# Where the modulation of a normalised input is applied: on the input's rows, or on the filter's weights with a rank-one shift

## The chip, the cores and the metric

The kernel runs on one core of one Trainium2 chip. The metric is the device time of one execution in microseconds (us); lower is better. A core has engines that run their own instruction streams in order and wait for each other by semaphores: TensorE (PE in the profile; PEld is its weight load), VectorE (DVE), ScalarE (ACT), GpSimd (POOL) and SyncE (SP, which here only issues DMAs).

## The reference

The kernel computes one block of a network in float32 on 2048 positions of 512 columns. The part that matters here is its first half: a layer norm of `u` is modulated by column vectors `ca` and `sa`, run through a long convolution whose kernel K is built from 128 complex states a column (S4), given a skip term, and added back under a gate `ga`.

```python
mod = (_silu(c) @ w_mod).reshape(c.shape[0], 6, 1, -1)
sa, ca, ga, sb, cb, gb = (mod[:, 0], ..., mod[:, 5])
h = _layernorm(x, axis=-1) * (1 + ca) + sa
x = x + ga * _A_ref(h, ...)
...
# _A_ref: K[d, l] = Re sum_n C[d,n] exp(dt[d] A[d,n] l) dt[d] B[d,n]
#         y = causal convolution of h with K (by FFT) + h * Dskip
```

The second half (a spatial shift mixer and a channel MLP) is not touched by the change. All of `ca`, `sa`, `ga` are one row of 512 numbers: they depend on the column, not on the position. The convolution and the skip are linear and act on each column by itself.

## The kernel before

The convolution is done as a Fourier transform in three stages: a 32-point transform over one index of the position, a twiddled 64-point one, a product of spectra, and the way back. The code runs in stages, each written out in order by hand (no scheduler moves instructions between or within engines; the order of the code is the order of each engine's queue). The stage of this case is a loop of 32 steps k, between the preparation of the constants and the second transform stage. It does two things side by side:

- **The filter.** For eight groups t of 64 columns (the `k // 4` of the code) and four quarters it builds the convolution kernel's partial sums. `turns(k)` computes phases on TensorE (L458, L459: two row halves of the array at once, 18 matmuls for a step), and ScalarE takes their sine and cosine (tile `tr`). `exps(t)` computes magnitudes: TensorE (L257, L252), then ScalarE's exponential. It is called in the steps with k % 4 == 1, and needs two loads of ScalarE's function table; there, a few filler matmuls (L492) stand between, and a dummy sine (`turn1`) brings the sine table back. `products(k)` multiplies magnitudes and phases on VectorE (L476, L482, L485, L486; tiles e, m). `burst(k)` sums over the states on TensorE (L508: 64 small matmuls into PSUM tile `kp`), and ScalarE copies every second `kp` into `KX`. The weight of each state, `WN`, enters by `weigh(t)` (L264), one multiplication of a quarter of the magnitudes' factors.
- **The input.** For each of 16 row blocks b, `u_stats` takes mean and variance on VectorE and the inverse root on GpSimd, and `u_norm` normalises and modulates in place by two instructions on VectorE (L425, L426). For every second block and each of two halves cp2, `u_dft` does the 32-point transform on TensorE (L435) into two PSUM banks; ScalarE copies them out (tile `vs`) and SyncE's queue writes them to DRAM (`VU`).

Step k emits, in this order: the copies left over from the step before; `turns(k + 2)`; the first two `exps` where there are any; `products(k)`; `burst(k)`; the rest of the `exps` with fillers; then the side work that a table assigns to the step (`side[k]`): norms, statistics, transforms. Block i is normalised in step 1 + 28 i // 16, its statistics two steps earlier, its transforms one and two steps later. Buffers tie the engines together: the phases use two PSUM buffers (`psx`), the sines three (`tr`), the products two, and the transforms of u share two PSUM banks (`psu`) with a few others.

Ahead of the loop, `mod_parts` and `mod_sum` make the column vectors `mods[0..2]` = sa, 1 + ca, ga, the same in all 128 partitions, in the order ca, ga, sa. The state weights are computed in `wn`, transposed on TensorE into a PSUM bank `wps`, and copied to `WN` by ScalarE. In step 1 the gate is multiplied into the scale and the shift (L584, L585), so that u comes out as ga (1 + ca) LN(u) + ga sa. The skip weights lie in four rows of the tile `DS` and are added into the filter's first tap at the end of the loop (`add_skip`).

Of the kernel before, what the change touches and what calls it, by code (L numbers as in the profile page):

```python
# [7 lines left out]
F32 = mybir.dt.float32  # L8
F32R = mybir.dt.float32r
# [18 lines left out]
def shape_constants():  # L28
    f = lambda x: np.ascontiguousarray(x.astype(np.float32))
    k1, k2, q = np.arange(32), np.arange(64), np.arange(32)  # L30
    c2b = lambda c: np.where(c < 32, 31 - c, c)
    th = 2 * np.pi * (k1[None] + .5) * q[:, None] / 64
    W = np.stack([np.cos(th), -np.sin(th)], 1)
    FU = np.zeros((4, 32, 2, 2, 2, 32))
    for h in range(2):
        for cp2 in range(2):
            cp = 2 * h + cp2
            FU[1 - cp if cp < 2 else cp, :, h, cp2] = W
    FU = FU.reshape(128, 2, 2, 2, 32).transpose(0, 1, 2, 4, 3)
    FK = np.zeros((2, 2, 32, 2, 64))  # L40
    FK[:, 0, :, 0] = FK[:, 1, :, 1] = W.reshape(32, 64)
    b = c2b(np.arange(64))
    al = 2 * np.pi * b[:, None, None] * ((k1[None, :, None] + .5) / 4096 + k2[None, None, :] / 64)
    c, s = np.cos(al), np.sin(al)
    T2 = np.stack([np.stack([c, -s], 2), np.stack([s, c], 2)]).reshape(128, 32 * 128)
    T3 = np.stack([s, -s]).reshape(128, 32 * 64)
    h, cq, cp2 = np.meshgrid(np.arange(2), np.arange(16), np.arange(2), indexing='ij')
    b = c2b((2 * h + cp2) * 16 + cq).reshape(64)
    al = 2 * np.pi * b[None, :] * k2[:, None] / 64
    c, s = np.cos(al), np.sin(al)  # L50
    Gm = np.zeros((64, 2, 64, 2))
    Gm[:, 0, :, 0], Gm[:, 0, :, 1], Gm[:, 1, :, 0], Gm[:, 1, :, 1] = c, s, -s, c
    Gm = np.tile(Gm.reshape(64, 256), (2, 1))
    FI = np.zeros((2, 2, 32, 16, 2, 2, 32))
    for hh in range(2):
        for c2 in range(2):
            for cc in range(16):
                bb = int(c2b(np.array((2 * hh + c2) * 16 + cc)))
                th = 2 * np.pi * (k1[:, None] + .5) * (bb + 64 * q[None]) / 4096
                FI[c2, 0, :, cc, hh, bb // 16 - 2 * hh] = np.cos(th) * (2 / 4096)  # L60
                FI[c2, 1, :, cc, hh, bb // 16 - 2 * hh] = -np.sin(th) * (2 / 4096)
    eye = np.eye(16)
    j = np.arange(32)
    c0 = np.tile((eye[:, :, None] * (j + .5)).reshape(16, 512), (2, 1))
    C0 = np.zeros((2, 2, 32, 2, 512))
    C0[:, 0, :, 0], C0[:, 1, :, 1] = c0, c0
    C0 = C0.reshape(128, 1024)
    e1 = (eye[:, :, None] * j).reshape(16, 512)
    e2 = (eye[:, :, None] * np.ones(32)).reshape(16, 512)
    C1 = np.concatenate([e1, e1, e2, e2] * 2, 0)  # L70
    ex0 = np.concatenate([np.arange(31, -1, -1), np.arange(32, 64)])
    ex1 = np.concatenate([64 * np.arange(8), 512 * np.arange(4)])
    CE = np.concatenate([(eye[:, :, None] * ex0.reshape(2, 32)[:, None, None, :]).transpose(1, 0, 2, 3).reshape(16, -1),
                         np.zeros((16, 64 * NX1))], 1)
    CE = np.tile(CE, (8, 1))
    for u in range(4):
        CE[u * 32:u * 32 + 32, 1024 + u * 16 * NX1:1024 + (u + 1) * 16 * NX1] = \
            np.tile((eye[:, :, None] * ex1).reshape(16, -1), (2, 1))
    PA = np.zeros((2, 4, 16, 2, 2, 4, 2, 16))
    PB = np.zeros((4, 2, 16, 4, 4, 2, 4, 16))  # L80
    for e in range(16):
        for v in range(2):
            for u in range(4):
                for p in range(2):
                    PA[v, u, e, v, p, u, p, e] = 1
        for c in range(8):
            for p in range(4):
                PB[c // 2, c % 2, e, c // 4 * 2 + c % 2, p, 1 - c // 2 % 2, p, e] = 1
    return {k: f(v) for k, v in dict(
        FU=FU.reshape(128, 256), FK=FK.reshape(128, 128), T2=T2, T3=T3, G=Gm,  # L90
        FI=FI.reshape(128, 16 * 128), C0=C0, C1=C1, CE=CE, PA=PA.reshape(128, 512), PB=PB.reshape(128, 2048), ID=np.eye(128)).items()}


# [18 lines left out]
def body(ctx, tc, A):  # L112
# [86 lines left out]
    MG = ph.tile([128, 512], F32R, name="MG")  # L199
    ON = ph.tile([128, 3, 128], F32R, name="ON")  # L200
    WN = ph.tile([128, 512], F32, name="WN")
    modu = ph.tile([128, 3, 512], F32, name="modu")
    mods = [modu[:, k] for k in range(3)] + [modg[:, k] for k in range(3)]
    psx = a1.enter_context(pool("psx", bufs=2, space=PSUM))
# [80 lines left out]
    with tc.manual_schedule():  # L285
# [13 lines left out]
        for j in range(4):  # L299
            Y.dma_start(DS[32 * j:32 * j + 1], A["dk"][j:j + 1])  # L300
        Y.dma_start(FK, A["FK"])
        V.memset(cst, MAGIC)
        for r in (32, 96):
            V.memset(cst[r:r + 32], 1.0)
# [101 lines left out]
        V.tensor_mul(ws, ws, mn)  # L406
        V.tensor_add(wn, wn, ws)
        V.tensor_tensor(as4(wn), as4(wn), by(dt), op=OP.mult)
    pr.close()

    wml = a1.enter_context(pool("wml", bufs=1, reuse_waits="tile"))
# [10 lines left out]
    def u_norm(b):  # L422
        x = ut[b // 4][:, b % 4]
        mv, r = ul.pop(b)
        V.scalar_tensor_tensor(x, x, mv[:, 0, 0:1], mods[1], op0=OP.subtract, op1=OP.mult)  # L425
        V.scalar_tensor_tensor(x, x, r[:, 0:1], mods[0], op0=OP.mult, op1=OP.add)  # L426

    def u_dft(b, cp2):
        x = ut[b // 4]
        ps = [psu.tile([128, 512], F32, name="pu") for h in range(2)]  # L430
        for i in range(2):
            for h in range(2):
                q = 64 * (1 - i if h == 0 else i)
                j = slice(32 * JB[2 * h + cp2], 32 * JB[2 * h + cp2] + 32)
                T.matmul(ps[h][q:q + 64], FU[j, h, cp2 * 64:cp2 * 64 + 64], x[j, b % 4 + i],  # L435
                         start=True, stop=True, skip_group_check=True)

        def evict():
            vs = uv.tile([128, 2, 512], F32, name="vs")
            for h in range(2):  # L440
                act(vs[:, h], ps[h])
                c0 = h * 32 + cp2 * 16 + (14 - b if h == 0 else b)
                for i in range(2):
                    Y.dma_start(dram(VU, (c0 + i) * 256, [[16384, 64], [1048576, 2], [1, 256]]),
                                vs[i * 64:i * 64 + 64, h].rearrange("p (a d) -> p a d", a=2))
        later.append(evict)
# [22 lines left out]
    def products(k):  # L469
# [5 lines left out]
        for a in range(2):  # L475
            V.scalar_tensor_tensor(e0[:, 1, a], tr[:, 1, 0], 1.0 - 2.0 * a, mg[:, a], op0=OP.mult, op1=OP.mult)  # L476
        if k == 0:
            weigh(0)
        if u % 2 == 0:
            m1 = m1s[0] = wk1.tile([128, 2, 512], F32, name="m1")  # L480
# [59 lines left out]
    with tc.manual_schedule():  # L540
# [2 lines left out]
        wps = psu.tile([128, 512], F32, name="pu")  # L543
        for i in range(4):
            T.transpose(wps[:, i * 128:i * 128 + 128], wn[:, i * 128:i * 128 + 128], ident)
        act(WN, wps)
        late = mod_parts(2)
        turns(1, 0)
        late()
# [4 lines left out]
        for k in range(33):  # L554
# [26 lines left out]
                if k % 4 == 3 and k < 28:  # L581
                    weigh(k // 4 + 1)
            if k == 1:
                V.tensor_mul(mods[1], mods[1], mods[2])  # L584
                V.tensor_mul(mods[0], mods[0], mods[2])  # L585
            for f in side[k]:
                f()
        for f in later:
# [681 lines left out]
```

## Time and profile before

| | us |
|---|---|
| median of 3 runs | 716.0 (714.89 to 717.39) |
| the profiled execution | 714.44 |
| its span, first to last instruction | 712.6 |

| engine | busy us | share of the span |
|---|---|---|
| TensorE, matmul | 669.5 | 94% |
| TensorE, weight load | 516.9 | 73% |
| VectorE | 506.6 | 71% |
| ScalarE | 335.5 | 47% |
| GpSimd | 86.7 | 12% |

The profiled execution's own time is 1.8 us above its span. The shares are means over stages: the loop of this case lies between about 40 and 212 us, and after it come the second stage of the transforms and the matmuls of the second half. A row of the order of time reads: start in us, duration, engine, line, operation, output<-input, shape, count, and in brackets the idle time of the engine before it and what ended it. A row of a group reads: line, engine, operation, output<-input, shapes, xcount | busy us, mean ns of one | idle us before them, and who ended it. A row of the waits reads: engine, tile and line <- the one waited for: us in total, times, longest. A row of a stretch reads: from:to, its length, the busy time and count of each engine, the clock granted to TensorE (1.00 is full), the share of the DMA engines and GB/s.

### The profile page before, as it was taken

The page shows a single profiled execution, that of the slowest core. Times are in us where ns is not written, and L with a number is a line of the kernel's source. Part 1 is how long each engine was busy: PE and PEld are TensorE (multiplying, and loading weights), DVE is VectorE, ACT ScalarE, POOL GpSimd, SP SyncE. Part 2 cuts the span into 40 slices and gives each one's busy share as a digit, 9 for nine tenths or more (in the row PEclk, how much of TensorE's full clock was granted, in tenths as well). Part 3 has the DMA queues.
Part 4 walks back from the last instruction along what each step waited for, and adds up shares of the span by engine and source line. Part 5 has one row for each costly group of instructions (what it writes and reads, how often), then busy time and mean ns, then how long its engine had stood idle before and what let it go on. Part 6 is the DMA issues. An engine that isn't in the chain of part 4 may idle for free.

```text
span 712.6 us, 16838 instructions
## 1 busy us (share of the span) xinstructions
PE 669.5 (94%) x7083; PEld 516.9 (73%) x7083; DVE 506.6 (71%) x847; ACT 335.5 (47%) x549; POOL 86.7 (12%) x191
## 2 busy tenths in 40 slices
PE   2689999999999999998999899999999999999997
PEld 1256555656569665664688889999898988989896
DVE  8889999999996666866988868557464636454422
ACT  3769888889866444533344623314123221212120
POOL 1011211112000000000473100101010000000000
PEclk9899999999999999999999999999999999999999
DMA  8451374653439999874659201011020101111011
GB/s 280 145 144 52 91 218 101 181 139 94 141 75 332 237 301 302 267 241 152 204 176 319 90 22 39 16 45 31 27 63 16 53 22 31 31 30 30 0 30 30
DMA packets 56627, 85.51 MB, mean 120 GB/s; under 512 B 5508, under 2 KB 43400, under 8 KB 54888
## 3 DMA queue, kind: packets, MB, share of 16 engines
q1 hardware_dynamic: 52536, 66.87, 33.2%
q0 software_dynamic: 3136, 16.52, 6.5%
q8 instruction: 56, 0.92, 0.6%
q10 hardware_dynamic: 880, 1.05, 0.5%
q14 instruction: 19, 0.16, 0.1%
HBM read 58.20 MB, written 31.85 MB: 126 GB/s over the span
## 4 chain that ended last, share of the span: by engine, by line
PE 47%; DMA 2%; DVE 2%; ACT 1%; issue 1%; SPq 1%; ACTq 0%; DVEq 0%
PE pm L824 7%; PE pm L825 7%; PE pm L827 7%; PE pa L948 6%; PE pa L940 6%; PE pa L941 6%; PE ph L878 2%; PE ph L879 2%; PE ph L881 2%; PE pT L789 2%; DMA ld<-ZT 1%; DMA GD<-go 1%; PE pT L1138 1%; PE py L721 1%; DMA win<-GD 0%
## 5 line engine op out<-in xcount | busy, mean ns | idle before, releaser
L120 ACT ACTIVATE gh<-pm 128x512 fp32r<-128x512 f32 (+1 forms) x48 | 26.9, 561 | 200.6 <-PE pm L827 200.6
L824 PE MATMUL pm<-nh,w3h 128*128 128x256 f32 (+1 forms) x352 | 85.8, 279 | 0.9 <-ACT nh L120 0.9
L825 PE MATMUL pm<-nh,w3l 128*128 128x256 f32 (+1 forms) x352 | 85.6, 279 | 0.1
L932 DVE TENSOR_TENSOR gl<-gf,gh 128x512 fp32r<-128x512 f32 (+1 forms) x48 | 30.9, 643 | 68.3 <-ACT gf L120 68.3
L940 PE MATMUL pa<-w4h,gh 128*128 128x512 f32 (+1 forms) x176 | 69.6, 395 | 0.0
L941 PE MATMUL pa<-w4l,gh 128*128 128x512 f32 (+1 forms) x176 | 68.9, 392 | 0.0
L824 PEld LDWEIGHTS pm<-nh,w3h 128*128 128x128 f32 (+1 forms) x352 | 65.3, 185 | 2.6 <-ACT nh L120 1.1
L825 PEld LDWEIGHTS pm<-nh,w3l 128*128 128x128 f32 (+1 forms) x352 | 65.2, 185 | 2.2 <-DVE w3l L743 0.5
L827 PE MATMUL pm<-nl,w3h 128*128 128x256 f32 (+1 forms) x352 | 54.8, 277 | 0.0
L948 PE MATMUL pa<-w4h,gl 128*128 128x512 f32 (+1 forms) x176 | 48.1, 390 | 0.8 <-DVE gl L932 0.8
L458 PE MATMUL xx<-MG,ON 64*128 64x512 f32 x160 | 47.0, 389 | 0.0
L459 PE MATMUL xx<-MG,ON 64*128 64x512 f32 x160 | 47.0, 389 | 0.0
L827 PEld LDWEIGHTS pm<-nl,w3h 128*128 128x128 f32 (+1 forms) x352 | 46.6, 185 | 0.2 <-DVE nl L797 0.2
L752 POOL TENSOR_TENSOR rs<-mv,eps_t 128x1 f32<-128x1 f32 (+1 forms) x39 | 11.9, 306 | 278.0 <-DVE mv L758 266.1
L884 DVE TENSOR_TENSOR h<-h,ph 128x512 f32<-128x512 f32 x16 | 11.0, 688 | 45.1 <-PE ph L881 45.1
L476 DVE SCALAR_TENSOR_TENSOR e<-tr,p 128x512 f32<-128x512 f32 x64 | 41.1, 683 | 1.8 <-ACT tr L120 1.8
L120 ACT ACTIVATE z<-pz 128x512 f32<-128x512 f32 x32 | 17.4, 594 | 51.4 <-issue 21.7
L677 DVE TENSOR_TENSOR ma<-pk,us 128x512 f32<-128x512 f32 x32 | 21.9, 686 | 26.8 <-issue 15.8
L508 PEld LDWEIGHTS kp<-e,e 128*32 128x32 f32 x2048 | 30.1, 110 | 12.9 <-issue 7.2
L948 PEld LDWEIGHTS pa<-w4h,gl 128*128 128x128 f32 (+1 forms) x176 | 33.0, 188 | 8.3 <-DVE gl L932 1.2
L485 DVE TENSOR_TENSOR e<-tr,p 128x1024 f32<-128x1024 f32 x32 | 39.0, 1218 | 0.0
L486 DVE TENSOR_TENSOR e<-tr,m 128x1024 f32<-128x1024 f32 x32 | 39.0, 1218 | 0.0
(234 smaller groups left out, 1755.6 us busy)
## 6 DMA issues: line engine op xcount, KB each, us to landing
VU<-vs SPq DMA_DIRECT2D x64, 128.0 KB, 3.2
ld<-VU SPq DMA_DIRECT2D x16, 512.0 KB, 14.1
ZT<-z POOLq DMA_DIRECT2D x15, 512.0 KB, 7.1
ld<-ZT SPq DMA_DIRECT2D x12, 512.0 KB, 5.5
Dw<-in_w POOLq DMA_DIRECT2D x8, 688.0 KB, 4.7
xu<-in_u SPq DMA_DIRECT2D x16, 256.0 KB, 5.7
KX<-in_u SPq DMA_DIRECT2D x16, 256.0 KB, 12.3
GD<-go SPq DMA_DIRECT2D x16, 256.0 KB, 2.5
```

What stands on the lines that cost most here:

```text
L120: return S.activation(out, in_, f, bias=bias, scale=scale)
L458: T.matmul(x[:, :512], la, ma, start=(i == 0), stop=(i == len(ops) - 1))
L459: T.matmul(x[:, 512:], lb, mb, start=(i == 0), stop=(i == len(ops) - 1))
L476: V.scalar_tensor_tensor(e0[:, 1, a], tr[:, 1, 0], 1.0 - 2.0 * a, mg[:, a], op0=OP.mult, op1=OP.mult)
L485: V.tensor_mul(e0[:, 0], tr[:, 0, 0:1].to_broadcast([128, 2, 512]), mg)
L486: V.tensor_mul(e1.rearrange("p r d q -> p r (d q)"), tr[:, :, 1], m1s[0][:, u % 2:u % 2 + 1].to_broadcast([128, 2, 512]))
L824: T.matmul(p, wh[:, k, c], hi[k], start=(k == 0), stop=False)
L825: T.matmul(p, wl[:, k, c], hi[k], start=False, stop=False)
L827: T.matmul(p, wh[:, k, c], lo[k], start=False, stop=(k == 3))
L940: T.matmul(acc[i], gh[:m, e, s], W4h[:m, f], start=(f == 0), stop=False)
L941: T.matmul(acc[i], gh[:m, e, s], W4l[:m, f], start=False, stop=False)
L948: T.matmul(acc[i], gl[:m, e, s], W4h[:m, f], start=False, stop=(f == 10))
```

## The change

u is now only normalised: (u - mean) r, by one instruction of ScalarE with a scale and a bias per row; VectorE forms the bias, -mean r, in one 128x1 instruction (`lun`). What depends on the column goes elsewhere:

- The factor ga (1 + ca) is multiplied into the state weights and into the skip weights. `mods[2]` becomes ga (1 + ca) ahead of the loop; a zero of 1 + ca is replaced by 1e-12 first. `WN` is made by a multiplication on VectorE out of PSUM, in step 0, in place of ScalarE's copy ahead of the loop. The four rows of `DS` are multiplied in step 1.
- The shift becomes sa / (1 + ca), to be added to the normalised u. It is the same for all positions, so that its 32-point transform is an outer product of the column sums of the transform's matrix (`F1`, a new constant) with the shift's row. One matmul for each of the two banks of `u_dft` writes this outer product first, and the transform accumulates on top of it. To keep float32's digits in the fast matmul format, row and sums are split into a rounded part and a rest, in rows 0, 32 and 64 of `SHS` and `F1S`, so that one matmul over 96 rows sums three products.
- `shift_rows`, called in step 1 in place of L584 and L585, makes the shift: reciprocal, multiplication, ScalarE's rounded copies, VectorE's rests.

```diff
+    F1 = np.zeros((96, 128))
+    F1[::32] = np.tile(W.sum(0).T.reshape(64), 2)
...
+        Y.dma_start(F1, A["F1"])
...
         V.tensor_tensor(as4(wn), as4(wn), by(dt), op=OP.mult)
+        V.tensor_scalar(ws, mods[1], 0.0, 1e-12, op0=OP.is_equal, op1=OP.mult)
+        V.tensor_add(mods[1], mods[1], ws)
+        V.tensor_mul(mods[2], mods[2], mods[1])
...
     def u_norm(b):
         x = ut[b // 4][:, b % 4]
         mv, r = ul.pop(b)
-        V.scalar_tensor_tensor(x, x, mv[:, 0, 0:1], mods[1], op0=OP.subtract, op1=OP.mult)
-        V.scalar_tensor_tensor(x, x, r[:, 0:1], mods[0], op0=OP.mult, op1=OP.add)
+        nm = wk.tile([128, 1], F32, name="lun")
+        V.scalar_tensor_tensor(nm, mv[:, 0, 0:1], -1.0, r, op0=OP.mult, op1=OP.mult)
+        act(x, x, AF.Identity, scale=r[:, 0:1], bias=nm)
+
+    def shift_rows():
+        V.reciprocal(mods[1], mods[1])
+        V.tensor_mul(mods[0], mods[0], mods[1])
+        act(SHS, mods[0][:96])
+        V.tensor_sub(SHS[64:96], mods[0][64:96], SHS[64:96].bitcast(F32))
+        act(F1S, F1)
+        V.tensor_sub(F1S[32:64], F1[32:64], F1S[32:64].bitcast(F32))
 
     def u_dft(b, cp2):
...
+        for h in range(2):
+            T.matmul(ps[h], F1S, SHS, start=True, stop=False, skip_group_check=True)
         for i in range(2):
             for h in range(2):
...
-                         start=True, stop=True, skip_group_check=True)
+                         start=False, stop=True, skip_group_check=True)
...
         if k == 0:
+            by_d = lambda z: z.rearrange("p (b a c) -> p b a c", b=32, a=4)
+            V.tensor_mul(by_d(WN), by_d(wps), mods[2].rearrange("p (a b c) -> p b a c", a=4, b=32))
             weigh(0)
...
-        act(WN, wps)
...
             if k == 1:
-                V.tensor_mul(mods[1], mods[1], mods[2])
-                V.tensor_mul(mods[0], mods[0], mods[2])
+                shift_rows()
+                for j in range(4):
+                    r = slice(32 * j, 32 * j + 1)
+                    V.tensor_mul(DS[r], DS[r], mods[2][r, j * 128:j * 128 + 128])
```

The queues of the engines move at three places. The numbers behind a tile's name are those of buffers, and in the brackets stands which engine's signal an instruction waits for. The line numbers of the changed kernel are a little higher: L476 becomes L496, L486 becomes L508, L508 becomes L530, L435 becomes L455.

VectorE's queue in step 1, before: the last product of step 1, the two multiplications of the column vectors, the normalisation of block 0, and the first product of step 2.

```order
L486 TENSOR_TENSOR e_553<-tr,m_467 128x1024
L584 TENSOR_TENSOR modu<-modu 128x512
L585 TENSOR_TENSOR modu<-modu 128x512 [waits Activation_49]
L425 SCALAR_TENSOR_TENSOR xu<-xu,lum,modu 128x512 [waits DVE_49,PE_49]
L426 SCALAR_TENSOR_TENSOR xu<-xu,lur,modu 128x512 [waits DVE_49,Pool_49]
L476 SCALAR_TENSOR_TENSOR e_639<-tr,p_264 128x512 [waits PE_49,Activation_49]
```

The same place in the changed kernel:

```order
L508 TENSOR_TENSOR e_560<-tr,m_474 128x1024
L439 RECIPROCAL modu<-modu 128x512
L440 TENSOR_TENSOR modu<-modu 128x512 [waits DVE_49,Activation_49]
L442 TENSOR_TENSOR SHS<-modu,SHS 32x512 [waits Activation_49]
L444 TENSOR_TENSOR F1S<-F_113,F1S 32x128 [waits DMAHW1_49,Activation_49]
L608 TENSOR_TENSOR DS<-DS,modu 1x128 x3
L608 TENSOR_TENSOR DS<-DS,modu 1x128 [waits DMAHW7_49]
L435 SCALAR_TENSOR_TENSOR lun<-lum,lur 128x1 [waits Pool_49]
L496 SCALAR_TENSOR_TENSOR e_655<-tr,p_268 128x512 [waits PE_49]
```

Between the products of step 1 and step 2, VectorE now has eight instructions of the new shift and skip, two of which wait for copies of ScalarE, and then the 128x1 bias.

ScalarE's queue at the same place of the changed kernel, from the exponentials of step 1 (tiles p) over the table load and the dummy sine to the phases of step 4 (`tr`):

```order
L122 ACTIVATE p_610<-xx 128x1024 [waits DVE_49,PE_49]
L122 ACTIVATE p_548<-xx 128x768 [waits PE_49]
L122 ACT_TABLE_LOAD
L122 ACTIVATE turn_377<-hpi 128x1
L122 ACTIVATE SHS<-modu 96x512 [waits DVE_49]
L122 ACTIVATE F1S<-F_113 96x128 [waits DMAHW1_49]
L122 ACTIVATE xu<-xu,lun,lur 128x512 [waits DMAHW5_49,DMAHW4_49,DMAHW6_49,DMAHW3_49,DVE_49]
L122 ACTIVATE KX<-kp 128x8x64
L122 ACTIVATE tr<-xx 128x1024 [waits PE_49,Activation_49]
```

Before, KX followed the dummy sine at once; SHS, F1S and the normalisation of block 0 (`xu`) have moved in between, and behind them wait the sines of step 4.

TensorE's queue in step 3 of the changed kernel, from the burst to the phases of step 6:

```order
L530 MATMUL kp<-e_728,e_729 32x64 x32
L450 MATMUL pu<-SHS,F1S 128x512 x2
L455 MATMUL pu<-xu,FU 64x512 x4
L478 MATMUL xx<-C_105,T0S 128x512
L479 MATMUL xx<-C_106,T1S 128x512
```

The row with SHS and F1S is new, here and ahead of each of the other 15 transforms of u; the rows around it stand as before.

More of the change, by code (lines that the diff above doesn't have):

```diff
@@ L89, in shape_constants @@
     return {k: f(v) for k, v in dict(
-        FU=FU.reshape(128, 256), FK=FK.reshape(128, 128), T2=T2, T3=T3, G=Gm,
+        FU=FU.reshape(128, 256), F1=F1, FK=FK.reshape(128, 128), T2=T2, T3=T3, G=Gm,
         FI=FI.reshape(128, 16 * 128), C0=C0, C1=C1, CE=CE, PA=PA.reshape(128, 512), PB=PB.reshape(128, 2048), ID=np.eye(128)).items()}
@@ L201, in body @@
     WN = ph.tile([128, 512], F32, name="WN")
+    F1 = ph.tile([96, 128], F32, name="F1")
+    F1S = ph.tile([96, 128], F32R, name="F1S")
+    SHS = ph.tile([96, 512], F32R, name="SHS")
     modu = ph.tile([128, 3, 512], F32, name="modu")
```

## The prediction

> **What bounds the kernel now.** I first read the busy shares by stretches, to find the stage that the change touches: the loop over 32 steps, from about 45 to 212 us. The first row below is its middle, the other three are a spell near the start in which TensorE idled.
>
> ```profile
> core 0: us, PE busy (x) PEld busy (x) DVE busy (x) ACT busy (x) POOL busy (x), PEclk, DMA share, GB/s
> 60.00:200.00 140.00, 135.20 (x2364) 84.42 (x2364) 137.91 (x181) 125.02 (x150) 24.51 (x36) 1.00 0.49 133
> 27.57:30.99 3.42, 0.33 (x1) 0.30 (x2) 3.28 (x7) 3.39 (x6) 0.00 (x0) 1.00 0.00 0
> 30.99:34.40 3.41, 3.17 (x4) 0.67 (x2) 2.31 (x4) 0.91 (x3) 0.00 (x0) 0.50 0.17 43
> ```
>
> In 140 us VectorE is busy 137.9, TensorE 135.2, ScalarE 125.0. The share alone names VectorE, and the change takes work from it. Whether that pays depends on who waits for whom, so next come the order of time for one step and the table of waits. A step k on TensorE is: the phases of step k+2 (18 matmuls of L458/L459), the burst of 64 small matmuls (L508) that needs VectorE's products (L476 to L486) of step k, and in 16 of the steps one DFT of u (L435).
>
> ```profile
> 105.55 1.22 DVE L486 TENSOR_TENSOR e<-tr,m 128x1024 f32<-128x1024 f32 x1
> ...
> 107.12 0.49 PE L458 MATMUL xx<-C,T0S 64*128 64x512 f32 x1
> ...
> 108.84 0.39 PE L458 MATMUL xx<-MG,ON 64*128 64x512 f32 x1
> ...
> 109.07 0.39 PE L458 MATMUL xx<-C0N,T0S 64*128 64x512 f32 x1
> ...
> 109.38 1.10 PE L508 MATMUL kp<-e,e 128*32 128x64 f32 x64
> ...
> 110.42 1.09 PE L435 MATMUL pu<-xu,FU 32*64 32x512 f32 x8
> ...
> 111.43 0.50 PE L458 MATMUL xx<-C,T0S 64*128 64x512 f32 x1
> ```
>
> The burst of step 11 starts at 109.38, 2.6 us after VectorE finished its products (106.77): TensorE was not waiting for VectorE, it was busy with the phases. From 107.12 to 111.43 the step is 2.26 us of phases, 1.04 of burst, 1.01 of DFT, with no gap. The waits over 60 to 200 us say the same:
>
> ```profile
> ACT vs L120 <- PE pu L435: 5.0, 7, 1.5
> ACT tr L120 <- PE xx L459: 3.5, 6, 1.1
> PE xx L257 <- ACT tr L120: 2.7, 6, 0.5
> PE xx L458 <- ACT p L120: 1.0, 3, 0.3
> PE kp L508 <- DVE e L486: 0.7, 2, 0.4
> ```
>
> TensorE loses 0.7 us to VectorE in the whole stretch. It and VectorE are about equally loaded; TensorE is in order and nearly gapless. So what the change adds to TensorE counts in full, and what it takes from VectorE is worth next to nothing.
>
> **The change, term by term.**
>
> *Work taken from VectorE.* Sixteen pairs of normalisation go:
>
> ```profile
> L426 DVE SCALAR_TENSOR_TENSOR xu<-xu,lur,modu 128x512 f32<-128x512 f32 x16 | 12.0, 752 | 1.8
> L425 DVE SCALAR_TENSOR_TENSOR xu<-xu,lum,modu 128x512 f32<-128x512 f32 x16 | 11.9, 746 | 0.0
> L168 DVE SCALAR_TENSOR_TENSOR dt_p<-dt_p,dt_r 128x8 f32<-128x8 f32 x6 | 1.0, 166 | 0.2
> ```
>
> A pair is 1.5 us, the 128x1 instruction in its place about 0.17 (nearest: 128x8, 166 ns): 16 x 1.33 = 21.3 us less VectorE. On the path this is worth only the waits of bursts for products: 0.7 us as recorded, about 1.1 with what a wait adds before the record shows it. **Term: -1.1** (bounds 0 and -2).
>
> *Outer products on TensorE.* Each of the 16 DFTs gets two matmuls of 96 rows x 128 columns x 512 ahead of it. The nearest work is the filler (L492), the same size and also placed behind a burst:
>
> ```profile
> 55.16 1.10 PE L508 MATMUL kp<-e,e 128*32 128x64 f32 x64
> 56.19 0.96 PE L492 MATMUL kp<-CE,TES 128*128 128x512 f32 x3
> 57.08 0.73 PE L257 MATMUL xx<-CE,TES 32*128 32x512 f32 x2
> ```
>
> Three fillers hold the engine 0.89 us, from 56.19 to 57.08. Inside a run one phase pair follows another every 0.23 us (108.84, 109.07); two fillers are thus 0.89 - 0.23 = 0.66, the switch between tile shapes included. Low end: 2 x 0.23 = 0.46; high end 0.89. I take 0.66, since they too stand between a burst and a narrow matmul: 16 x 0.66 = **+10.5** (7.4 to 14.2). Nothing covers it, as the step above has no gap.
>
> *The stop in step 1.* After the products of step 1 VectorE now runs `shift_rows`: a reciprocal, a multiplication, then a subtraction that needs ScalarE's copy SHS. In ScalarE's order that copy stands behind the five exponentials of step 1, a table load and the dummy sine. Behind the waiting subtraction are queued on VectorE the F1S subtraction, four skip rows, the small instruction, and the products of step 2. The place before, in the order of time of VectorE, ScalarE and TensorE, and below them the prices:
>
> ```profile
> 51.13 0.68 DVE L584 TENSOR_TENSOR modu<-modu 128x512 f32<-128x512 f32 x1
> ...
> 53.86 1.29 DVE L476 SCALAR_TENSOR_TENSOR e<-tr,p 128x512 f32<-128x512 f32 x2
> ...
> 57.34 1.22 DVE L486 TENSOR_TENSOR e<-tr,m 128x1024 f32<-128x1024 f32 x1
> ...
> 60.82 1.28 DVE L476 SCALAR_TENSOR_TENSOR e<-tr,p 128x512 f32<-128x512 f32 x2
> ...
> 64.29 0.42 DVE L264 TENSOR_TENSOR p<-p,WN 128x256 f32<-128x256 f32 x1
> ```
> ```profile
> 61.98 0.20 ACT L120 ACTIVATE turn<-hpi 128x1 f32<-128x1 f32 x1
> 62.09 0.58 ACT L120 ACTIVATE KX<-kp 128x512 f32<-128x512 f32 x1
> ```
> ```profile
> 62.27 1.10 PE L508 MATMUL kp<-e,e 128*32 128x64 f32 x64
> 65.98 1.10 PE L508 MATMUL kp<-e,e 128*32 128x64 f32 x64
> ```
> ```profile
> L372 DVE RECIPROCAL tp_mx<-tp_mx 128x512 f32<-128x512 f32 x1 | 3.4, 3353 | 0.0
> L304 DVE MEMSET cst<- 32x512 f32 x2 | 1.0, 485 | 0.3 <-DVE cst L302 0.2
> L309 DVE MEMSET cst<- 1x128 f32 x6 | 1.0, 165 | 0.4
> ```
>
> VectorE would be done with reciprocal and multiplication (3.35 + 0.69) at about 55.5. ScalarE reaches SHS at 62.1, where KX stood, and needs 0.6: 62.7. Then the subtraction on 32 partitions (0.49 to 0.69, taken 0.65), F1S 0.2, four rows of 128 at about 0.2, the small instruction 0.17: the products of step 2 start at 64.5 instead of 53.86. They took 58.56 - 53.86 = 4.70, so they end at 69.2, and the burst that ran at 62.27 runs at 69.25: +7.0. Step 3 follows: small instruction, statistics (0.82) and products (60.82 to 64.29, 3.47) end at 73.7, while TensorE is ready at 69.25 + 1.03 + 2.3 = 72.6. Its burst moves from 65.98 to 73.75. In step 4 the products end at 78.65 and TensorE arrives at 78.7: the debt is paid, TensorE is the later one again and catches nothing up. **Term: +7.8.** Bounds: +4 (if VectorE's small instructions overlap and ScalarE gets there earlier) and +10.
>
> *The clock.* TensorE then idles some 7 us. The granted clock fell to 0.50 from 30.99 to 34.40, after the 3.42 us before it held only 0.33 of matmul; while it is low, matmuls take twice as long, up to 1.7 us lost, but the wait of step 3 (1.1 us) hides most. **Term: +0.5** (0 to 1.7). The Trainium skill (TensorE: Matmul & The Clock Gate, Part 1) states that after at least one idle window of about 3.4 us the clock is halved until a busy window has passed; the row agrees, one window long. By that rule alone the sum would have 1.7 in place of 0.5.
>
> *ScalarE.* It gets 16 normalisations of 128x512, about 0.6 us by the nearest row, and loses one eviction (WN) before the loop:
>
> ```profile
> L120 ACT ACTIVATE vs<-pu 128x512 f32<-128x512 f32 x32 | 17.5, 604 | 6.3 <-PE pu L435 6.3
> ```
>
> That is 9.6 us into 15 us of idle time per 140, much of it ScalarE waiting for the very DFTs that get longer by 0.66. It has slack where they stand (TensorE's waits for ScalarE, 2.7 + 1.0, sit at the exponentials). **Term: 0** (0 to +5).
>
> *Ahead of the loop.* Three more VectorE instructions on the columns (0.43 + 0.69 + 0.69) follow the weights, in an idle spell of 1.84 us:
>
> ```profile
> 38.00 0.69 DVE L408 TENSOR_TENSOR KX<-KX,dt_o 128x512 f32<-128x512 f32 x1
> 40.53 1.29 DVE L476 SCALAR_TENSOR_TENSOR e<-tr,p 128x512 f32<-128x512 f32 x2 [1.84 <-ACT tr L120]
> 42.19 0.43 DVE L264 TENSOR_TENSOR p<-p,WN 128x256 f32<-128x256 f32 x1 [0.37 <-ACT WN L120]
> ```
> ```profile
> 44.88 1.12 PE L228 MATMUL pu<-xu,sp 128*128 128x512 f32 x2 [1.66 <-ACT xu L120]
> ```
>
> WN is now VectorE's multiplication out of PSUM: about 0.3 later than ScalarE's copy. A burst here starts 3.7 us after its products (58.56 to 62.27 in step 2, below called the lead), which covers it; were that gone, 0.3. The PSUM bank is held until 42.5, and its next user on TensorE comes at 44.9. F1 is one small load more on SyncE's queue, early. **Term: 0.**
>
> *Sum.* -1.1 + 10.5 + 7.8 + 0.5 = +17.7. Behind the loop nothing absorbs it: the next stage starts from the loop's last result. Against the profiled execution's own 714.4 us that gives 732.1. The runs' median is 1.6 above it; I forecast **733**.
>
> **Rivals.**
>
> *VectorE is the bound (faster).* If TensorE's 135 us held hidden slack, the loop would follow VectorE: -21.3, plus 4.5 for `shift_rows` beyond the two multiplications it replaces and 0.3. ScalarE would stop the gain at 125.0 + 14 x 0.6 = 133.4 of 140, so -6.6 there: about 708. It decides if bursts start right at the end of their products; step 11 speaks against it with 2.6 us. The Trainium skill (Perfetto Trace Analysis, Identifying the Most-Contended Engine) holds that TensorE's headroom is judged by weight loads, not matmul time; at 84.4 of 140 it would name VectorE. The gapless step decides against it here. Chance 0.05.
>
> *The stop is absorbed.* Had VectorE's delay stayed under the 3.7 us of that lead, only 10.5 - 1.1 would remain: 725. The order of both engines speaks against it. Chance 0.12.
>
> *ScalarE becomes a second bound.* In the steps with exponentials its table loads and sines already hold TensorE up; eight normalisations fall in or beside them, 8 x 0.6 = +5: 738. Chance 0.13.
>
> **Numbers.** The main case has 0.68 (727 to 737 by its terms' bounds); 0.02 is left for no change. About 0.3% (2 us) is what a measurement of this kernel can tell. Faster 0.05, same 0.02, slower 0.93. The range 724 to 740 takes in the absorbed stop and the ScalarE case and leaves out the fast one and the joint extremes.
>
> **What would show it.** In the profile after: a TensorE gap of about 7 us near 62 us ended by VectorE's products, with VectorE idle from 55.5 to 62.7 waiting for ScalarE's SHS; steps with a DFT of about 4.95 us instead of 4.31; VectorE's share of the loop falling to about 80% with TensorE unchanged; the loop's last burst near 230 instead of 212. Wrong would be: no such gap, outer products that take under 0.4 us a pair, or bursts that start as soon as their products end.

## The result

The changed kernel takes 735.1 us (median of four runs, 732.6 to 737.7), against 715.7 us for the kernel before: the ratio is 1.0268, with a 95% interval of 1.0228 to 1.0309. The forecast was 733, within 724 to 740.

The profile after, first by the shares of busy time from step 2 to the end of the norms, then two stretches around the place where the prediction saw a stop.

```profile
core 0: us, PE busy (x) PEld busy (x) DVE busy (x) ACT busy (x) POOL busy (x), PEclk, DMA share, GB/s
60.00:217.00 157.00, 145.40 (x2391) 90.36 (x2390) 126.61 (x178) 135.98 (x167) 23.57 (x36) 0.98 0.41 118
62.20:67.95 5.75, 0.53 (x6) 0.10 (x2) 4.73 (x11) 3.50 (x8) 0.00 (x0) 1.00 0.00 1
67.95:74.78 6.83, 4.64 (x78) 3.88 (x80) 6.79 (x11) 2.19 (x3) 1.89 (x3) 0.50 0.29 99
```

VectorE has fallen from 98% of the loop (137.9 of 140) to 81% (126.6 of 157), and the loop has become longer. The stop in the order of time, VectorE first:

```profile
50.04 1.22 DVE L508 TENSOR_TENSOR e<-tr,m 128x1024 f32<-128x1024 f32 x1
51.18 3.35 DVE L439 RECIPROCAL modu<-modu 128x512 f32<-128x512 f32 x1
54.63 0.69 DVE L440 TENSOR_TENSOR modu<-modu 128x512 f32<-128x512 f32 x1
63.10 0.68 DVE L442 TENSOR_TENSOR SHS<-modu,SHS 32x512 fp32r<-32x512 f32 x1 [7.79 <-ACT SHS L122]
63.80 0.28 DVE L444 TENSOR_TENSOR F1S<-F,F1S 32x128 fp32r<-32x128 f32 x1
64.10 1.19 DVE L608 TENSOR_TENSOR DS<-DS,modu 1x128 f32<-1x128 f32 x4
65.32 0.16 DVE L435 SCALAR_TENSOR_TENSOR lun<-lum,lur 128x1 f32<-128x1 f32 x1
...
68.87 1.22 DVE L508 TENSOR_TENSOR e<-tr,m 128x1024 f32<-128x1024 f32 x1
```

ScalarE at the same place, where the copy SHS stands behind the exponentials (p; two more run just ahead of the first row), the table load and the dummy sine (turn):

```profile
58.22 2.82 ACT L122 ACTIVATE p<-xx 128x1024 f32<-128x1024 f32 x3 [0.15 <-PE xx L262]
61.05 1.28 ACT L122 ACT_TABLE_LOAD   x1
62.35 0.20 ACT L122 ACTIVATE turn<-hpi 128x1 f32<-128x1 f32 x1
62.46 0.61 ACT L122 ACTIVATE SHS<-modu 96x512 fp32r<-96x512 f32 x1
```

And TensorE, with the two outer products (L450) between burst and transform:

```profile
70.14 1.93 PE L530 MATMUL kp<-e,e 128*32 128x64 f32 x64 [7.42 <-DVE e L508]
...
75.55 1.10 PE L530 MATMUL kp<-e,e 128*32 128x64 f32 x64
76.58 0.73 PE L450 MATMUL pu<-SHS,F1S 96*128 96x512 f32 x2
77.25 1.09 PE L455 MATMUL pu<-xu,FU 32*64 32x512 f32 x8
...
80.56 1.10 PE L530 MATMUL kp<-e,e 128*32 128x64 f32 x64
```

VectorE stands still for 7.8 us until ScalarE has made SHS, and TensorE then stands still for 7.4 us until the products of step 2 are there. From 76.58 to 77.25 the two outer products hold TensorE 0.67 us.

Where the 19 us come from is read best from the start of the bursts (L508 before, L530 after), one a step, taken from the two traces:

| burst of step | before, us | after, us | later by | outer products before it | later by, without 0.67 us for each pair |
|---|---|---|---|---|---|
| 0 | 49.92 | 50.27 | 0.35 | 0 | 0.35 |
| 2 | 62.27 | 70.14 | 7.87 | 0 | 7.87 |
| 3 | 65.98 | 75.55 | 9.57 | 0 | 9.57 |
| 5 | 76.55 | 87.47 | 10.92 | 2 | 9.58 |
| 16 | 136.46 | 150.87 | 14.41 | 8 | 9.05 |
| 31 | 212.02 | 231.18 | 19.16 | 16 | 8.44 |

Nearly all of it arises in two ways: 9.6 us at once in steps 2 and 3, and then about 0.67 us at each transform of u. The fall of the last column from 9.58 to 8.44 comes for the most part at the bursts of steps 12 and 24 (0.42 and 0.48), where before the burst waited for VectorE's products, and otherwise in steps that have exponentials beside the transform, where a pair adds only some 0.47. Behind the loop the two kernels differ by less than 1 us (500.6 and 501.5 us to the end of the span).

### The profile page after: what moved, and what is told of

Same layout as the page of the kernel before. It is cut to its first block, busy times and chain, and to the rows that moved or that the text cites. A ratio compares the mean times of both kernels' runs of the same rounds, so it can differ in the third digit from the quotient of the medians.

```text
span 732.7 us, 16909 instructions
## 1 busy us (share of the span) xinstructions
PE 683.7 (93%) x7115; PEld 525.8 (72%) x7115; DVE 494.2 (67%) x841; ACT 346.9 (47%) x566; POOL 85.6 (12%) x191
## 4 chain that ended last, share of the span: by engine, by line
PE 46%; DMA 2%; DVE 2%; ACT 1%; issue 1%; SPq 0%; ACTq 0%; DVEq 0%
PE pm L847 7%; PE pm L848 7%; PE pm L850 7%; PE pa L971 5%; PE pa L963 5%; PE pa L964 5%; PE ph L901 2%; PE ph L902 2%; PE ph L904 2%; PE pT L812 2%; PE py L744 1%; DMA GD<-go 1%; PE pT L1161 1%; DMA ld<-ZT 1%; DMA win<-GD 0%
## 5 line engine op out<-in xcount | busy, mean ns | idle before, releaser
L496 DVE SCALAR_TENSOR_TENSOR e<-tr,p 128x512 f32<-128x512 f32 x64 | 41.1, 684 | 23.2 <-ACT tr L122 18.1
L478 PE MATMUL xx<-MG,ON 64*128 64x512 f32 x160 | 48.4, 399 | 0.0
L479 PE MATMUL xx<-MG,ON 64*128 64x512 f32 x160 | 48.2, 398 | 0.0
L530 PEld LDWEIGHTS kp<-e,e 128*32 128x32 f32 x2048 | 30.8, 112 | 19.4 <-DVE e L508 8.6
L530 PE MATMUL kp<-e,e 128*32 128x64 f32 x2048 | 36.1, 223 | 7.4 <-DVE e L508 7.4
L508 DVE TENSOR_TENSOR e<-tr,m 128x1024 f32<-128x1024 f32 x32 | 39.0, 1218 | 0.0
```

Source lines behind the costliest of these rows:

```text
L478: T.matmul(x[:, :512], la, ma, start=(i == 0), stop=(i == len(ops) - 1))
L479: T.matmul(x[:, 512:], lb, mb, start=(i == 0), stop=(i == len(ops) - 1))
L530: T.matmul(kp[32 * j:32 * j + 32, (k % 2) * 4 + g], e1[:, r, d], e0[:, r, :, d * 32:d * 32 + 32], start=(r == 0), stop=(r == 1), skip_grou ...
```

## The experiments

All ratios are to the kernel before, from runs on the same chip beside it. Where an experiment is told by its bursts, these are taken from its trace as in the table above.

### The two costs, taken away one at a time and together

The first run takes the wait out of VectorE's step 1: the rests are subtracted in step 2, the skip rows multiplied in step 5.

```diff
         act(SHS, mods[0][:96])
-        V.tensor_sub(SHS[64:96], mods[0][64:96], SHS[64:96].bitcast(F32))
         act(F1S, F1)
+
+    def shift_rests():
+        V.tensor_sub(SHS[64:96], mods[0][64:96], SHS[64:96].bitcast(F32))
         V.tensor_sub(F1S[32:64], F1[32:64], F1S[32:64].bitcast(F32))
...
             if k == 1:
                 shift_rows()
+            if k == 2:
+                shift_rests()
+            if k == 5:
                 for j in range(4):
```

> The subtractions of the two rests move from step 1 to step 2 and the four skip rows to step 5, so that VectorE no longer waits for ScalarE's copies ahead of the products of step 2; all else is as in the changed kernel. My theory: the stop costs 9.6 us (bursts of steps 3 to 5 stand 9.6 us late after the outer products before them are taken off), so the gap of TensorE near 62 us goes, and the time is 735.1 - 9.6 = 725.5 us (723 to 728), 1.4% over the kernel before. Rival, ScalarE: its 16 normalisations of 0.81 us lengthen the loop, and the stop only hides some of it; then less than 5 us come back, and the time is over 730.

Measured: 727.6 us, ratio 1.0188 (1.0132 to 1.0243), the profiled span 723.4 against 732.7: inside the range of 723 to 728, but 7.5 us come back and not 9.6. TensorE's order of time shows what is left:

```profile
62.26 1.10 PE L532 MATMUL kp<-e,e 128*32 128x64 f32 x64
65.03 0.50 PE L480 MATMUL xx<-C,T0S 64*128 64x512 f32 x1 [1.67 <-ACT tr L122]
...
68.22 1.10 PE L532 MATMUL kp<-e,e 128*32 128x64 f32 x64 [0.77 <-DVE e L510]
```

The burst of step 2 is back at 62.26, where it was before the change. The burst of step 3 is at 68.22 in place of 65.98, for two reasons. Ahead of its phases TensorE waits 1.67 us for sines of ScalarE (before the change 0.26, at the same place): in ScalarE's queue SHS, F1S and the normalisation of block 0 now stand ahead of them. And the burst itself waits 0.77 us for VectorE's products, since the wait for ScalarE's copy, which comes at 62.7 whatever VectorE does, has moved by one step:

```profile
58.97 1.22 DVE L510 TENSOR_TENSOR e<-tr,m 128x1024 f32<-128x1024 f32 x1
62.71 0.68 DVE L445 TENSOR_TENSOR SHS<-modu,SHS 32x512 fp32r<-32x512 f32 x1 [2.52 <-ACT SHS L122]
```

The second run leaves the outer products out (and with them the shift), and keeps the stop.

```diff
-        for h in range(2):
-            T.matmul(ps[h], F1S, SHS, start=True, stop=False, skip_group_check=True)
...
-                         start=False, stop=True, skip_group_check=True)
+                         start=True, stop=True, skip_group_check=True)
```

> The 32 outer products are left out (the shift is thus missing from the result); the stop in step 1 stays. My theory: they stand on a gapless TensorE, 16 x 0.67 = 10.7 us, so the time is 735.1 - 10.7 = 724.4 us (722 to 727). Rival, VectorE or ScalarE as the loop's bound: the outer products lie beside other work, and under 4 us come back, over 731.

Measured: 723.7 us, ratio 1.0137 (1.0069 to 1.0205), inside the range. By the medians 11.4 us come back; the steps with a transform take 4.31 us again where they took 4.98 (step 16). By the last burst it is 8.0 us (223.17 against 231.18): in step 10 of this trace the granted clock falls (0.82 from 107.5 to 117.0 us) and the burst comes 1.6 us later, which neither the kernel before nor the changed one shows. Without that it would be 9.6. The outer products stand nearly in full on TensorE.

The third run has both edits.

> Both of the two edits: no outer products (the shift is missing from the result) and the rests taken later. What is left of the change is VectorE's relief of 21 us and ScalarE's 16 normalisations. My theory: TensorE alone sets the loop, VectorE's relief is worth about 1 us and ScalarE's load nothing: 735.1 - 9.6 - 10.7 = 714.8 us (712 to 717), equal to the kernel before within its uncertainty. Rival, VectorE was the bound: 708 or less. Rival, ScalarE: 719 or more.

Measured: 718.7 us, ratio 1.0073 (1.0040 to 1.0107): slower than before, by 3 to 4 us that my theory had not (712 to 717 was the range). By the bursts it is level at step 2 (62.23), 2.2 late at step 3, 2.8 late at step 4 (73.12 against 70.30) and 2.9 at step 31 (214.93 against 212.02). So the rest arose in steps 3 and 4, and not along the loop, as 16 normalisations on ScalarE would have it. As in the first run, it has two parts: TensorE waits 1.64 us for ScalarE's sines in step 3 (0.26 before), and the bursts of steps 3 and 4 wait 0.79 and 0.55 us for VectorE's products. A later run takes the second part away.

### The outer products alone

In the first, each outer product is made twice.

```diff
-        for h in range(2):
-            T.matmul(ps[h], F1S, SHS, start=True, stop=False, skip_group_check=True)
+        for n in range(2):
+            for h in range(2):
+                T.matmul(ps[h], F1S, SHS, start=True, stop=False, skip_group_check=True)
```

> Each outer product is made twice (the second writes the same values over the first). My theory: two more matmuls on TensorE without cover, of 0.23 to 0.34 us each as nothing changes shape between them: 16 x 0.46 to 16 x 0.67, so 742.5 to 745.8 us. Rival, VectorE or ScalarE as the bound: under 739.

Measured: 740.7 us, ratio 1.0359 (1.0317 to 1.0400), 5.6 us over the changed kernel: below the range of 742.5 to 745.8, above the rival's 739. TensorE:

```profile
149.24 1.10 PE L531 MATMUL kp<-e,e 128*32 128x64 f32 x64
150.27 1.20 PE L451 MATMUL pu<-SHS,F1S 96*128 96x512 f32 x4
151.39 1.09 PE L456 MATMUL pu<-xu,FU 32*64 32x512 f32 x8
...
154.69 1.10 PE L531 MATMUL kp<-e,e 128*32 128x64 f32 x64
```

Four hold TensorE 1.12 to 1.15 us where two held 0.67, and the step takes 5.45 in place of 4.98: 0.47 for the second pair, the low end. The first pair costs 0.20 more than the second. The change of the tile shape behind the burst may be the reason; no run here tests that. The last burst is 7.05 us later than in the changed kernel (16 x 0.47 = 7.5); the run as a whole, only 5.6. The difference is of the size by which the medians wander, and I take the trace for it.

The other run puts the outer products alone into the kernel before, of tiles that hold zeros.

```diff
+    F1S = ph.tile([96, 128], F32R, name="F1S")
+    SHS = ph.tile([96, 512], F32R, name="SHS")
...
     def u_dft(b, cp2):
...
+        for h in range(2):
+            T.matmul(ps[h], F1S, SHS, start=True, stop=False, skip_group_check=True)
...
-                         start=True, stop=True, skip_group_check=True)
+                         start=False, stop=True, skip_group_check=True)
```

> The kernel before, with nothing of the change but the two outer products ahead of each transform of u, of tiles that hold zeros, so that they add nothing. My theory: TensorE alone sets the loop, and 16 x 0.67 = 10.7 us come on top of 714.9: 724.6 to 726.5, with some of the 1 us of waits for VectorE gone. Rival, VectorE is the bound of the kernel before and TensorE has slack beside it: less than 5 us, under 720.

Measured: 727.5 us, ratio 1.0170 (1.0136 to 1.0203), so 12 us (9.7 to 14.5 by the interval), a little above the range. VectorE is as laden as ever and there is no stop, and the steps with a transform again take 0.66 to 0.67 us longer (0.46 to 0.50 in the three that have exponentials too). The last burst is 10.4 us later than before (222.44 against 212.02). Two things in this number are not the matmuls themselves. The waits for VectorE's products at the bursts of steps 12 and 24 are gone here too (0.43 and 0.48 us), though VectorE has lost no work: TensorE merely comes later. And 1.0 us arises ahead of the burst of step 25, at a gap of TensorE that no engine's signal ends:

```profile
190.94 0.50 PE L465 MATMUL xx<-MG,ON 64*128 64x512 f32 x1 [0.71 <-issue]
```

### VectorE's relief alone

The kernel before without its 32 normalising instructions (u goes raw into its transform).

```diff
     def u_norm(b):
...
-        V.scalar_tensor_tensor(x, x, mv[:, 0, 0:1], mods[1], op0=OP.subtract, op1=OP.mult)
-        V.scalar_tensor_tensor(x, x, r[:, 0:1], mods[0], op0=OP.mult, op1=OP.add)
```

> The kernel before, with the 32 instructions of the normalisation (L425, L426) left out, so that u goes raw into its transform: VectorE has 24 us less to do in the loop, and nothing else changes. My theory: bursts wait for products about 1 us in all, so 713 to 715 us against 714.9. Rival, VectorE is the bound: the loop follows it until TensorE's or ScalarE's load stops it, at least 6 us less, under 709.

Measured: 714.0 us, ratio 0.9980 (0.9961 to 0.9998). VectorE has lost 24 us, and the kernel about 1:

```profile
60.00:200.00 140.00, 135.60 (x2367) 84.48 (x2365) 117.48 (x148) 125.70 (x151) 21.44 (x35) 1.00 0.49 133
```

VectorE is busy 117.5 of 140 us, against 137.9 with the same TensorE and ScalarE, and the stretch holds the same work. Relieving an engine at 98% was worth 1 us. The rule of the Trainium skill (Perfetto Trace Analysis, Identifying the Most-Contended Engine) that TensorE's headroom is read from weight loads, beside the share of the peak arithmetic (not worked out here), would have made TensorE, at 84.5 of 140, the one with room; here the measurement decides against it.

### The rest of the stop, and the change at its best

Both kernels take the rests in step 3, behind its products, and the skip rows in step 5. One leaves the outer products out (and the shift), the other leaves out nothing. Against the third and the first run above only this differs:

```diff
-            if k == 2:
+            if k == 3:
                 shift_rests()
```

> As the run without outer products and with the rests taken in step 2 (the shift is missing from the result here too), but the rests are taken in step 3, behind its products. In that run the copies of ScalarE came only at 62.7 us, after the products of step 2 (60.2), so VectorE still waited 2.5 us and the bursts from step 3 on stood 2.5 to 2.9 us late; from there to the end of the loop the two kernels kept step. My theory: that wait is all that was left, and the time is that of the kernel before, 714 to 716 us. Rival, ScalarE's 16 normalisations: it stays at 718 or more.

Measured: 716.7 us, ratio 1.0018 (0.9994 to 1.0042): no difference from before that can be told, though the trace has one. From the burst of step 0 to that of step 31 this kernel takes 163.55 us, the third run 165.08, the kernel before 162.10. So the moved wait was half of what the third run had left. The other half stands here too, in step 3, first this kernel, then the one before:

```profile
63.72 0.50 PE L478 MATMUL xx<-C,T0S 64*128 64x512 f32 x1 [1.63 <-ACT tr L122]
```
```profile
63.63 0.50 PE L458 MATMUL xx<-C,T0S 64*128 64x512 f32 x1 [0.26 <-ACT tr L120]
```

TensorE waits 1.4 us longer for the sines, and that is the time of SHS, F1S and the first normalisation ahead of them on ScalarE. Between step 4 and step 31 the bursts of this kernel stand 141.78 us apart, before 141.72, though VectorE is relieved by 21 us and ScalarE carries the norms. The waits at steps 12 and 24 are gone; in their place TensorE has one new wait for a sine, and the burst of step 27 behind it comes 0.6 us later:

```profile
195.85 0.50 PE L478 MATMUL xx<-C,T0S 64*128 64x512 f32 x1 [0.34 <-ACT tr L122]
```

> The changed kernel with the rests taken in step 3 and the skip rows in step 5, with its outer products: nothing left out. My theory: the outer products alone remain, 714.8 + 10.7 = 725.5 us less the 1 us of waits for VectorE: 724 to 726.5, the best that this change can do. Rival, something else of the change lengthens the loop: 728 or more.

Measured: 726.9 us, ratio 1.0158 (1.0127 to 1.0188). That is just above the range and below the rival's 728. The last burst is at 222.44, where the kernel before with nothing but idle outer products has it. That the two agree to the hundredth is chance: this kernel has 1.65 us of the wait for sines in step 3, the other one the gap ahead of step 25. What remains of the change is the outer products and, by the trace, those 1.4 us of ScalarE, which the medians cannot tell.

### The shift on GpSimd, a way around TensorE

Since GpSimd is nearly idle, three kernels let it add the shift row to the normalised u, in place of the outer products. The first also forms the reciprocal there.

```diff
         V.tensor_mul(mods[2], mods[2], mods[1])
+        P.tensor_tensor(mods[1], mods[1], m_one[:, 0:1].to_broadcast([128, 512]), op=OP.pow)
...
         act(x, x, AF.Identity, scale=r[:, 0:1], bias=nm)
+        P.tensor_tensor(x, x, mods[0], op=OP.add)
...
     def shift_rows():
-        V.reciprocal(mods[1], mods[1])
-        V.tensor_mul(mods[0], mods[0], mods[1])
...
+        P.tensor_tensor(mods[0], mods[0], mods[1], op=OP.mult)
...
-        for h in range(2):
-            T.matmul(ps[h], F1S, SHS, start=True, stop=False, skip_group_check=True)
```

> The changed kernel with the shift added to the normalised u by GpSimd (one 128x512 addition a block) in place of the outer products; GpSimd also forms the reciprocal (a power of -1, before the loop) and the shift, so that VectorE has nothing of shift_rows; the skip rows are multiplied in step 5. My theory: both costs of the change go, TensorE has the queue of the kernel before, and the time is that of before less up to 1 us: 713.5 to 716. Two things could add: GpSimd's addition is late for the transform one step after the steps with exponentials (up to 1 us in each of three), and VectorE slows down while GpSimd works; with either 717 to 722.

Measured: 787.6 us, ratio 1.1003 (1.0974 to 1.1033). One instruction did it:

```profile
L417 POOL TENSOR_TENSOR modu<-modu,m_one 128x512 f32<-128x512 f32 x1 | 82.0, 81950 | 30.6 <-DVE modu L416 30.6
```

The power over 512 columns takes 82 us, GpSimd's roots for the norms wait behind it, and VectorE stands still for 69.4 us ahead of the first `lun`. The burst of step 2 is 67 us late. The forecast is missed by 72 us, and the run says little on the theory beyond that.

The next is the same without the fillers of the steps with exponentials (`fill(3)` and `fill(1)` in the loop taken out).

> The same as the run with the shift on GpSimd, without the five filler matmuls of each of the seven steps with exponentials (35 in all). If TensorE is the bound, its steps with exponentials get shorter until ScalarE's exponentials (0.98 us each against 1.09 of TensorE's pairs with filler) set the pace: about 0.3 us in each of seven, so 2 us less than that run, 711.5 to 714. Rival: the clock falls in the gaps that the fillers covered, and the time is above that run's.

Measured: 800.9 us, ratio 1.1183 (1.1152 to 1.1215), 13 us more than with the fillers. The stretch of 50 us in which both have settled, without and with the fillers:

```profile
195.00:245.00 50.00, 47.76 (x724) 28.34 (x722) 42.31 (x57) 44.51 (x54) 18.50 (x20) 0.84 0.45 129
```
```profile
195.00:245.00 50.00, 49.03 (x828) 30.47 (x831) 45.75 (x59) 47.57 (x61) 18.95 (x20) 1.00 0.44 129
```

The granted clock averages 0.84 in place of 1.00, and from step 18 on the steps next to the exponentials take 10 to 11 us in place of 7.7. The forecast is missed, and the rival stated for this run holds: here the clock falls without the fillers, and the time is above that run's.

The third leaves reciprocal and shift on VectorE in step 1 and normalises each block, from the second on, a step earlier.

```diff
-        side[at(i)].append(lambda i=i: u_norm(i))
+        side[max(at(i) - 1, 1)].append(lambda i=i: u_norm(i))
```

> The changed kernel with the shift added to the normalised u by GpSimd in place of the outer products, as in the earlier run, but the reciprocal and the shift stay on VectorE in step 1, and each block from the second on is normalised one step earlier, so that GpSimd's addition (1.6 us) is done when the transform comes. VectorE's step 1 then has 4.0 us of reciprocal and multiplication and no wait, against 2.7 us of multiplications and normalisation before, within the 3.7 us of lead. My theory, TensorE with the queue of the kernel before sets the loop: 714 to 717 us, equal to the kernel before. Rival, VectorE slowed by GpSimd's additions (two of its instructions took 2.3 us in place of 1.2 while one ran) becomes the bound: 718 to 725.

Measured: 730.9 us, ratio 1.0207 (1.0169 to 1.0245). The rival's side, and worse than its 718 to 725. VectorE and GpSimd in the order of time:

```profile
68.09 1.22 DVE L498 TENSOR_TENSOR m<-p 128x1024 f32<-128x1024 f32 x1
68.48 1.98 POOL L436 TENSOR_TENSOR xu<-xu,modu 128x512 f32<-128x512 f32 x1 [1.72 <-ACT xu L122]
69.22 2.33 DVE L501 TENSOR_TENSOR e<-tr,p 128x1024 f32<-128x1024 f32 x1
```

While GpSimd's addition runs, the product takes 2.33 us in place of 1.22. The bursts of steps 16, 23 and 24 start 0.05 us after their products, that is they wait for VectorE, and their steps take 5.8 to 6.9 us in place of 3.8 to 4.3. Only part of that is slower products. VectorE also stands still, in six places for 22.2 us in all, until GpSimd has made the inverse root for the next bias; that root stands in GpSimd's queue behind an addition, and the addition waits for ScalarE's normalisation. Ahead of step 23:

```profile
188.49 0.16 DVE L434 SCALAR_TENSOR_TENSOR lun<-lum,lur 128x1 f32<-128x1 f32 x1 [7.88 <-POOL lur L153]
```

Steps 5 and 6 take 9.4 and 12.0 in place of 6.3 and 7.2, and there the clock is low while TensorE has work all the time:

```profile
74.00:94.40 20.40, 20.34 (x136) 11.56 (x132) 13.56 (x21) 12.82 (x16) 2.29 (x4) 0.50 0.15 39
```

Why it stayed low for so long is not shown. The profiled execution is the slowest of six (733.9; the others 726.9 to 732.5, at a higher mean clock), so the median's 16 us need not hold all of this. What each of the three costs was not taken apart by runs, and a version with the roots out of the additions' way was not tried. None of the versions tried beats the kernel before.

## Why the prediction was right, point by point

- **TensorE bounds the loop, VectorE does not** (term -1.1). Right for the relief alone: -1.1 us by the medians of the run without normalisation. The 0.4 us that the term adds to the recorded 0.7 stands in no row; what the relief gave at the two bursts that had waited, those of steps 12 and 24, is 0.41 and 0.48. Beside the outer products the term is in part counted twice, since these alone already end both waits. That the burst of step 11 started 2.6 us after its products was the row that told it, against a busy share of 98%.
- **Outer products** (term +10.5, from the filler). Right: 0.67 us a pair, +10.4 at the last burst in the kernel before with idle ones (1.0 of it the unrelated gap, and less the 0.9 of waits that went with them). The filler, between bounds of 0.46 and 0.89, was the right neighbour to price by: like the outer products it stands between a burst and a narrow matmul, while a second pair in the same place costs 0.47.
- **The stop in step 1** (term +7.8). The mechanism as told: VectorE waits for SHS until 63.1 (forecast 62.7), the burst of step 2 is 7.9 us late (forecast 7.0). Sized a little low: in step 3 the burst was forecast to be 7.8 us late and was 9.57, of which 1.1 are the clock (next point), so 8.5. Taking the rests from step 1 to step 3 and the skip rows to step 5 gives back 8.2 us (735.1 to 726.9), since the wait for sines in step 3, which the stop had covered, then shows.
- **The clock** (term +0.5). TensorE idled 7.4 us and the clock stood at 0.50 from 67.95 for 6.83 us. The burst took 1.93 us in place of 1.10, and the burst of step 3 started 1.1 us after its products, where the forecast had TensorE waiting for them. So about 1.1 in place of 0.5. The rule that was cited from the Trainium skill (TensorE: Matmul & The Clock Gate, Part 1) agrees with the idle spell; the low clock lasted two of its windows of about 3.4 us.
- **ScalarE** (term 0). In the changed kernel this came out, but by luck. The duration was mis-sized: a normalisation takes 0.81 us, not 0.6.

```profile
L122 ACT ACTIVATE xu<-xu,lun,lur 128x512 f32<-128x512 f32 x16 | 12.9, 809 | 3.7 <-DVE lun L435 3.7
```

  The Trainium skill (ScalarE: Activation LUTs, What ACT_TABLE_LOAD costs) counts some 93 ns for each operand read per partition on top of the plain instruction; with scale and bias both so, an estimate from its figures is 0.80, and the row agrees. The reason given for 0, that ScalarE has slack where the new work stands, fails in step 1: SHS, F1S and the first normalisation delay the sines, and TensorE waits 1.4 us longer for them as soon as the stop no longer covers that wait. From step 4 on, with the norms on ScalarE and no outer products, the loop gains nothing (141.78 against 141.72 us); without any norms it gains 0.96 (from 71.04 to 211.80, that is 140.76). So there ScalarE's load eats the little that VectorE's relief gives, by a sine that comes late for step 27; that is read from the trace and was not tested by a run of its own.
- **Ahead of the loop** (term 0). The three column instructions take 37.38 to 39.25 and the first product of step 0 follows at 39.31: no wait of VectorE there now. How this part stands to before cannot be read to better than 2 us, since the start of the loop moves by that much between executions (burst of step 0 at 48.6 to 50.6 in twelve of the thirteen traces; the one with the power has 52.2).
- **The sum and the range.** At the last burst the kernel is 19.2 us late, forecast 17.7: the stop was 0.7 low, the clock 0.6, the outer products and the relief together 0.2. The 727 to 737 given for the main case does not follow from its terms' bounds, which add up to 9.4 and 25.9 us without ScalarE's, that is 724 to 740.

Of the rivals, "VectorE is the bound" falls by the run without norms and by the one with idle outer products; "the stop is absorbed" by the burst of step 2; "ScalarE becomes a second bound", at +5 us, by the run with neither cost, which is within 0.4% of the kernel before; 1.4 us of ScalarE are in its trace all the same.

## What to carry to other kernels

An engine's share of busy time does not say that it bounds a stage: look at one step, and ask whether the consumer starts when the product ends. If it starts later, relieving the producer is worth what the few exceptions sum to (here 1 us of 24 taken away), and what is put on the consumer counts nearly in full.

When a long in-order queue gets a new instruction that waits for another engine, find the place of the awaited instruction in the other queue, not its duration: here a copy of 0.6 us cost 8, because it started 7.1 us after its input was ready, behind the exponentials and a table load. Moving the waiting half two steps on removed that. The copy itself still delayed what stood behind it in its own queue, by 1.4 us together with the two instructions next to it.

## What the runs showed of the hardware that was not expected

- A power on GpSimd over 128x512 takes 82 us, while an addition of the same size takes 1.3 to 2.2 us.
- A VectorE product of two tiles in SBUF takes 2.3 us in place of 1.2 while a GpSimd addition runs, as quoted above. In the rows the product ahead of it ends at 69.31, the addition (1.98 us there, 1.28 alone) at 70.46, and the slow product 1.09 us later: they go one after the other. The Trainium skill (SBUF — State Buffer, Who interferes with whom) states that a VectorE instruction with two SBUF inputs contends with a GpSimd instruction that reads SBUF, over a shared pair of ports that one of them locks; the rows agree.
- Two matmuls of 96x128x512 between a burst of 128x32 tiles and matmuls of 32x64 tiles cost 0.67 us, two more in the same place only 0.47. Whether the 0.20 is the price of a change of the tile shape was not tested.
